# Attention and a squared-ReLU MLP on one core: score visits of three pieces in place of two

## The chip, the cores and the metric

The kernel runs on one core of one Trainium2 chip. The metric is the time of one execution on the device in microseconds (us), taken over several runs. The core has a matrix engine, TensorE (PE in the profile, with PEld for its weight loads), the elementwise engines VectorE (DVE) and ScalarE (ACT), GpSimd (POOL), and SyncE (SP). SP issues most of the DMAs here; POOL issues those of the first two batches and of the weights.

## The reference

Two operations are fused. The first is causal attention over 8 batches, 8 heads, 576 queries and head size 64, with 16 extra "beacon" keys and values in front that every query may see. The second is an MLP on the 4608 rows that come out of it.

```python
k_all = np.concatenate([beacon_k, k], axis=2)          # 592 keys
v_all = np.concatenate([beacon_v, v], axis=2)
scores = scale * np.matmul(q, k_all.transpose(0, 1, 3, 2))
causal[:, Nb:] = np.triu(np.ones((S, S), dtype=bool), k=1)
scores = np.where(causal, -1e9, scores)
a = softmax(scores);  attn = np.matmul(a, v_all)
x = attn.transpose(0, 2, 1, 3).reshape(4608, 512)
h = np.maximum(x @ w_in, 0.0)                          # 512 -> 2048
out = (h * h) @ w_out                                  # 2048 -> 512
```

## The kernel before

**Attention.** The 8 heads are taken as 4 pairs per batch; pair number p is 4b + pr. Keys stand on partitions, so a score matmul has only the 64 rows of one head as its contraction. The two heads of a pair lie in partitions 0 to 63 and 64 to 127 of `qT` and `kT`, and `emit_scores` (L607) issues their matmuls alternately. The causal part of a pair's scores is laid out as a stream of 1664 columns (`STREAM`, L547), the stream of a batch is 4 × 1664 = 6656 columns, and `PIECES` cuts it into 13 pieces of 512 columns.

A **strip** is a PSUM tile of 128 × 2 × 512 fp32, which is two banks, one for each head. A **score visit** is one stay of PE on scores: in batches 1 to 7 `new_visit` (L630) and `add_batch` (L641) make visits of two pieces, with both strips, and a last one of one piece, so seven visits for a batch. One ACT instruction (`add_exp`, L618) then takes the exponential of a whole strip, both heads together (1024 columns), into the bf16 buffer `pt`. DVE applies the causal mask with a minimum (`emit_mask`, L689 and L693), PE multiplies by the values (L715; a column of ones gives the row sum), and DVE divides (L732, L734) into `xn`. Batch 0 goes by another, finer path (`add_pair`).

`xn` is transposed into `xT`, by PE for batches 0 to 2 (L782) and by DMA for the rest (`add_xt`, L765).

**MLP.** It runs over 9 chunks of 512 rows. Stage 1 (L878) is, for each of 16 column groups, four matmuls of 512 columns into one PSUM bank; ACT (L894) or DVE (L896) applies the ReLU into `g`, and DVE squares (L903). Stage 2 (L916) is, for each of four groups of 128 rows, sixteen matmuls into one bank; the result is copied to `osb` (L316 or L318) and stored by SP (L944). For the last rows it is cut into three column ranges (L828).

**PSUM.** All eight banks are given out: two strips (four banks) and four single banks `ps`, which serve the MLP, the value matmuls (two at most) and the transposes (two at most).

**What sets the order.** No queue is written out by hand. `Order.run` (L69) is a planner that runs while the program is built: every piece of work is an `Op` with an engine, a duration, what it needs, what it takes from a pool of buffers (`take`) and gives back (`give`), a priority and sometimes a gate. The planner simulates the engines, always starts the available op of lowest priority number, and emits the instructions in that order. On the chip each engine runs its instructions strictly in that order and waits on semaphores. A visit has a gate (`gate_at`, L598): it prefers to wait until the MLP has come so far. When PE has nothing to do in the first 22 us of the plan, the planner puts in fillers (L286): matmuls on zeros whose result nobody reads, of 128 columns up to 4.0 us of the plan and of 256 columns after that (L139).

The lines that fix the shape of a visit:

```python
    qk = add(f"qk{b}.{n}", "PE", 0.2, emit, prio=100.0 * pos - 1000.0, take=("strip", "strip"), gate=gate_at(pos - SHIFT))
    ...
    if len(parts) == 2 or n == NPC - 1 and b not in CROSS:
        opened.clear()
```

**Loads.** Batches 0 and 1 are loaded by POOL's queue, in strided form, and transposed by PE (L472, L475). From batch 2 on SP loads q, k and v into eight staging buffers (L362), POOL casts to bf16 (L318), and two large DMA transposes on SP write `qT` and `kT` (L395). SP also issues the `xT` transposes (L765) and the stores (L944), all in one queue.

Of the kernel before, what the change touches and what calls it, by code (L numbers as in the profile page):

```python
# [11 lines left out]
AF = mybir.ActivationFunctionType  # L12
# [4 lines left out]
class Op:  # L17
# [1 line left out]

    __slots__ = ("name", "engs", "dur", "emit", "prio", "need", "users", "left", "ready",  # L20
                 "take", "give", "gate", "held", "slots", "dma", "pe_time", "behind", "followers",
                 "sync", "insts", "late")

    def __init__(self, name, engs, dur, emit, prio=0.0, deps=(), take=None, give=None,
                 gate=None, dma=0.0, pe_time=0.0, behind=(), sync=(), late=0.0):
        self.name = name
        self.late = late
        self.engs = engs if isinstance(engs, (tuple, list)) else (engs,)
        self.dur = dur
        self.emit = emit  # L30
        self.prio = prio
        self.sync = list(sync)
        self.need = list(deps) + self.sync
        self.users = []
        self.take = (*take, 1)[:3] if take else None
        self.give = give
        self.gate = gate
        self.held = None
        self.slots = []
        self.dma = dma  # L40
        self.pe_time = pe_time
        self.behind = list(behind)
        self.followers = []


class Order:
# [16 lines left out]
    def add(self, *a, **kw):  # L63
        op = Op(*a, **kw)
        op.need = [d for d in op.need if d is not None]
        self.ops.append(op)
        return op

    def run(self):  # L69
# [23 lines left out]
        now = 0.0  # L93
        while events:
            now = events[0][0]
            while events and events[0][0] <= now + 1e-9:
                _, _, kind, op = heapq.heappop(events)
                if kind in ("done", "done_pe"):
                    for u in op.users:
                        if ("PE" in u.engs) == (kind == "done_pe"):  # L100
                            u.left -= 1
                            if u.left == 0:
                                release(u)
                elif kind == "give":
                    from_op, which = op.give if isinstance(op.give, tuple) else (op.give, 0)
                    pool, cls = from_op.take[:2]
                    self.pools[pool].append(from_op.slots[which])
                    if cls in self.inuse:
                        self.inuse[cls] -= 1
            again = True  # L110
            while again:
                again = False
                for e in engines:
                    if free[e] > now + 1e-9:
                        continue
                    best = None
                    fallback = None
                    for op in avail[e]:
                        if any(free[x] <= now + 1e-9 for x in op.engs[:op.engs.index(e)]):
                            continue  # L120
                        if op.take:
                            pool, cls, need = op.take
                            if len(self.pools[pool]) < need:
                                continue
                            if cls in self.limits and self.inuse[cls] + need > self.limits[cls]:
                                continue
                        if op.gate is not None and not op.gate(self):
                            if fallback is None or op.prio < fallback.prio:
                                fallback = op
                            continue  # L130
                        if op.dma and len(lanes[e]) >= self.DEPTH[e] and lanes[e][-self.DEPTH[e]] > now + 1e-9:
                            continue
                        if best is None or op.prio < best.prio:
                            best = op
                    if best is None:
                        best = fallback
                    if best is None:
                        if e == "PE" and 0.3 < now < self.FILL_UNTIL and self.pools["ps"]:
                            cols = 128 if now < 4.0 else 256  # L139
                            free[e] = now + 0.107  # L140
                            issued.append((Op("fill", "PE", 0.107, lambda e, cols=cols, bank=self.pools["ps"][0]: self.fill(bank, cols)), e, now))
                            seq += 1
                            heapq.heappush(events, (free[e], seq, "free", None))
                        continue
# [8 lines left out]
                    if op.take:  # L153
                        pool, cls, need = op.take
                        op.slots = [self.pools[pool].pop(0) for _ in range(need)]
                        op.held = (pool, cls, op.slots[0])
                        if cls in self.inuse:
                            self.inuse[cls] += need
                    dur = op.dur[e] if isinstance(op.dur, dict) else op.dur
# [34 lines left out]
def kernel(  # L194
# [403 lines left out]
    def gate_at(pos):  # L598
        return lambda o: o.progress >= mlp_chunk_us * (LEAD + PACE * (pos - HP))
# [7 lines left out]
    def emit_scores(b, mms, st):  # L607
        for pr, c, t0, t1, at in mms:
            for hj in range(2):
                hp = slice(64 * hj, 64 * hj + 64)  # L610
                nc.tensor.matmul(  # L611
                    st[:, hj, at:at + t1 - t0],
                    kT[b % 2][hp, pr, 128 * c:128 * c + 128],
                    qT[b % 2][hp, pr, t0:t1],
                    start=True, stop=True,
                )

    def add_exp(name, qk, s, at, width, prio):  # L618
        def emit(e):
            nc.scalar.activation(pt[:, :, at:at + width], strips[qk.slots[s]][:, :, 0:width],  # L620
                                 AF.Exp, bias=0.0, scale=scale)

        return add(name, "ACT", 0.18 + 2 * width / 1200.0, emit, prio=prio, deps=[qk], give=(qk, s))

    exps_of = {}
    CROSS = ()
    SHIFT = 0.25
    opened = []

    def new_visit(b, n):  # L630
        pos = HP * b + 512.0 * n / PW
        parts = []

        def emit(e):
            for s, (bb, m) in enumerate(parts):
                emit_scores(bb, PIECES[m], strips[qk.slots[s]])

        qk = add(f"qk{b}.{n}", "PE", 0.2, emit, prio=100.0 * pos - 1000.0, take=("strip", "strip"), gate=gate_at(pos - SHIFT))
        opened.append((qk, parts))

    def add_batch(b):  # L641
        for pr in range(HP):
            p = HP * b + pr
            qk_ops[p], av_ops[p], exps_of[p] = [], [], []
        for n in range(NPC):
            if not opened:
                new_visit(b, n)
            qk, parts = opened[0]
            parts.append((b, n))
            qk.take = ("strip", "strip", len(parts))  # L650
            qk.dur += sum(t1 - t0 for _, _, t0, t1, _ in PIECES[n]) / 2400.0
            pairs = sorted({mm[0] for mm in PIECES[n]})
            e = add_exp(f"exp{b}.{n}", qk, len(parts) - 1, 512 * n, 512,
                        1.0e-2 * (HP * b + 512.0 * n / PW) - 30.0)
            for pr in pairs:
                p = HP * b + pr
                for o in deps_of(b, pr, 0) + av_ops[p - HP]:
                    if o not in qk.need:
                        qk.need.append(o)
                qk_ops[p].append(qk)  # L660
                exps_of[p].append(e)
            if len(parts) == 2 or n == NPC - 1 and b not in CROSS:
                opened.clear()
        for pr in range(HP):
            add_phase(b, pr, HP * b + pr, 0, WHOLE[pr][0], 100.0 * (HP * b + pr), exps_of[HP * b + pr])

    def add_pair(b, pr):
        p = HP * b + pr
        qk_ops[p], av_ops[p] = [], []
        for n, ph in enumerate(SPLIT):  # L670
            base = 20.0 * RANK.index((p, n))
            exps = []
            for i, (mms, off, width) in enumerate(ph.pieces):
                def emit_qk(e, mms=mms, box=(box := {})):
                    emit_scores(b, [(pr, *mm) for mm in mms], strips[box["qk"].slots[0]])

                qk = box["qk"] = add(f"qk{p}.{n}.{i}", "PE", 0.2 + sum(max(96, mm[2] - mm[1]) for mm in mms) / 2400.0, emit_qk,
                                     prio=base + i - 1000.0, deps=deps_of(b, pr, n), take=("strip", "strip"))
                qk_ops[p].append(qk)
                exps.append(add_exp(f"exp{p}.{n}.{i}", qk, 0, PW * p + off, width, (base + i) * 1.0e-4 - 400.0))  # L680
            add_phase(b, pr, p, n, ph, base, exps)

    def add_phase(b, pr, p, n, ph, base, exps):
# [364 lines left out]
```

The softmax here doesn't subtract the row's maximum and nothing guards it: scores larger than these inputs give would overflow.

## Time and profile before

| what | value |
|---|---|
| median of 8 runs | 341.02 us (340.63 to 343.6) |
| the profiled execution, its own time | 341.17 us |
| the profiled execution, its span | 339.4 us |
| PE busy | 335.1 us |
| ACT busy | 190.3 us |
| DVE busy | 170.5 us |
| POOL busy | 93.2 us |
| score matmuls (L611) | 596 |
| exponentials (L620) | 107 |

The time of a run is longer than the span of its profile by 1.8 us, which lie around the instructions. Busy is the time in which an engine had at least one instruction at work. Matmuls are pipelined, and the record of one reaches beyond the start of the next; so the useful length of a PE stretch is read from the start of its first matmul to the start of the first matmul of the next stretch.

### The profile page before, as it was taken

The numbers are of one execution on the slowest core, as the hardware profiler recorded it, in microseconds if no ns is written. First come the engines' busy times: TensorE is split into PE (matmuls) and PEld (weight loads), VectorE is DVE, ScalarE is ACT, GpSimd is POOL, SyncE is SP. The second block draws the span as 40 slices with busy tenths as digits, with TensorE's granted clock in tenths as the row PEclk, the third lists the DMA queues.
The fourth block names the chain that finished last, engine by engine and source line by source line (L and its number), as shares of the span: only waits on it lengthen the run. The fifth ranks groups of instructions, "written<-read, shape, count | busy, mean of one in ns | idle before, by whom it ended". The sixth has DMA issues, their size and how long they took to land.

```text
span 339.4 us, 7787 instructions
## 1 busy us (share of the span) xinstructions
PE 335.1 (99%) x3197; PEld 187.2 (55%) x3197; DVE 170.5 (50%) x389; ACT 190.3 (56%) x270; POOL 93.2 (27%) x145
## 2 busy tenths in 40 slices
PE   8999999999999999999999999999999999999996
PEld 7578765544554554554458845545555544444444
DVE  3786976147465973486236643766255502401400
ACT  3886765377638745575466654665277216514621
POOL 9874803416405514052415051403000000000000
PEclk9999999999999999999999999999999999999999
DMA  8999989999899999899989998996310131011003
GB/s 149 189 206 218 206 145 196 232 240 216 173 211 231 201 174 185 180 229 171 211 156 222 231 206 135 215 229 121 105 62 2 29 104 62 0 61 64 0 2 124
DMA packets 143953, 51.72 MB, mean 152 GB/s; under 512 B 130702, under 2 KB 138798, under 8 KB 143918
## 3 DMA queue, kind: packets, MB, share of 16 engines
q1 hardware_dynamic: 135375, 42.19, 62.2%
q0 software_dynamic: 7904, 8.69, 14.9%
q8 instruction: 25, 0.41, 0.5%
q10 hardware_dynamic: 639, 0.36, 0.4%
q14 instruction: 10, 0.08, 0.1%
HBM read 37.22 MB, written 9.44 MB: 137 GB/s over the span
## 4 chain that ended last, share of the span: by engine, by line
PE 98%; DVE 1%; issue 0%; ACT 0%; DVEq 0%
PE ps L878 37%; PE ps L916 36%; PE ps L715 9%; PE strip L611 9%; PE ps L286 3%; PE ps L475 1%; PE ps L782 1%; PE ps L828 1%; DVE g L903 1%; PE ps L472 0%; PE ps L420 0%; DVE g L896 0%; ACT osb L316 0%; DVE g L292 0%; DVE qT L318 0%
## 5 line engine op out<-in xcount | busy, mean ns | idle before, releaser
L878 PE MATMUL ps<-xT,w_in 128*128 128x512 bf16 (+3 forms) x704 | 134.0, 340 | 0.1
L916 PE MATMUL ps<-w_out,g 128*128 128x512 bf16 x560 | 131.5, 379 | 0.0
L620 ACT ACTIVATE pt<-strip 128x1024 bf16<-128x1024 f32 (+3 forms) x107 | 101.9, 999 | 42.9 <-PE strip L611 42.5
L878 PEld LDWEIGHTS <-w_in 128*128 128x128 bf16 x704 | 65.5, 98 | 52.3 <-issue 1.4
L894 ACT ACTIVATE g<-ps 128x512 bf16<-128x512 f32 (+2 forms) x120 | 67.6, 563 | 43.9 <-PE ps L878 43.2
L903 DVE TENSOR_TENSOR g<-g 128x1024 bf16<-128x1024 bf16 (+2 forms) x80 | 52.6, 663 | 68.7 <-ACT g L894 67.8
L916 PEld LDWEIGHTS <-g 128*128 128x128 bf16 x560 | 51.0, 98 | 54.8 <-issue 1.7
L318 POOL CAST qk_area<-stg 128x512 bf16<-128x512 f32 (+2 forms) x60 | 41.7, 702 | 66.6 <-DMA stg<-in_q_dram 32.9
L316 ACT COPY osb<-ps 128x512 f32<-128x512 f32 (+2 forms) x28 | 15.8, 568 | 50.8 <-PE ps L916 48.6
L318 POOL CAST vb<-stg 128x512 bf16<-128x512 f32 (+1 forms) x40 | 25.5, 645 | 66.0 <-DMA stg<-in_v_dram 48.4
L715 PEld LDWEIGHTS <-pt 128*128 128x128 bf16 (+1 forms) x960 | 35.7, 98 | 11.0 <-issue 1.9
L715 PE MATMUL ps<-vb,pt 128*128 128x65 bf16 (+1 forms) x960 | 39.8, 194 | 0.0
L689 DVE TENSOR_TENSOR pt<-pt,tri 128x512 bf16<-128x512 bf16 x64 | 30.3, 483 | 10.5 <-ACT pt L620 9.4
L611 PE MATMUL strip<-qT,kT 64*128 64x208 bf16 (+15 forms) x596 | 34.2, 239 | 0.0
L734 DVE TENSOR_TENSOR xn<-ps,rcp 128x320 bf16<-128x320 f32 (+2 forms) x64 | 31.5, 492 | 2.3
L611 PEld LDWEIGHTS <-kT 64*128 64x128 bf16 x596 | 19.0, 94 | 21.2 <-issue 19.7
L732 DVE RECIPROCAL rcp<-ps 128x5 f32<-128x5 f32 (+2 forms) x64 | 12.2, 191 | 36.3 <-PE ps L715 36.2
L896 DVE TENSOR_SCALAR g<-ps 128x512 bf16<-128x512 f32 (+2 forms) x40 | 23.4, 602 | 8.4 <-PE ps L878 7.5
L318 DVE COPY osb<-ps 128x512 f32<-128x512 f32 (+1 forms) x10 | 6.5, 652 | 30.6 <-PE ps L916 15.2
L286 PE MATMUL ps<-g 128*128 128x256 bf16 (+1 forms) x83 | 11.8, 299 | 1.1 <-DVE warm L293 1.1
L362 POOL DMA_DIRECT2D stg<-in_v_dram x10 | 8.6, 866 | 5.8 <-DMA w_in<-in_moe_w_in_dram 4.2
L286 PEld LDWEIGHTS <-g 128*128 128x128 bf16 x83 | 7.8, 121 | 3.3 <-issue 1.4
(40 smaller groups left out, 82.5 us busy)
## 6 DMA issues: line engine op xcount, KB each, us to landing
out_dram<-osb SPq DMA_DIRECT2D x17, 512.0 KB, 4.2
stg<-in_q_dram SPq DMA_DIRECT2D x24, 256.0 KB, 4.9
stg<-in_k_dram SPq DMA_DIRECT2D x18, 256.0 KB, 5.2
stg<-in_v_dram SPq DMA_DIRECT2D x18, 256.0 KB, 4.8
w_in<-in_moe_w_in_dram POOLq DMA_DIRECT2D x4, 512.0 KB, 7.9
w_out<-in_moe_w_out_dram POOLq DMA_DIRECT2D x4, 512.0 KB, 10.8
stg<-in_v_dram POOLq DMA_DIRECT2D x6, 256.0 KB, 7.6
stg<-in_k_dram SPq DMA_DIRECT2D x6, 224.0 KB, 4.2
```

What stands on the lines that cost most here:

```text
L286: nc.tensor.matmul(ps[bank][:, 0:cols], g[1][:, 0, 0:128], g[1][:, 0, 0:cols], start=True, stop=True)
L318: eng[e].tensor_copy(dst, src)
L611: nc.tensor.matmul(st[:, hj, at:at + t1 - t0], kT[b % 2][hp, pr, 128 * c:128 * c + 128], qT[b % 2][hp, pr, t0:t1], start=True, stop=True,)
L620: nc.scalar.activation(pt[:, :, at:at + width], strips[qk.slots[s]][:, :, 0:width], AF.Exp, bias=0.0, scale=scale)
L689: nc.vector.tensor_tensor(out=d, in0=d, in1=tri[:, m0:m0 + m, :][:, None].to_broadcast([128, 2, m, 128]), op=ALU.min)
L715: nc.tensor.matmul(a[:, at + (t - tl[0]) * (D + 1):at + (t - tl[0] + 1) * (D + 1)], P[0:rr, hj, o:o + 128], vb[b % 2][0:rr, c, 2 * pr + hj ...
L734: nc.vector.tensor_tensor(out=xn[b % 2].rearrange("p t (h d) -> p h t d", d=D)[:, h0:h0 + nh, tl[0]:tl[0] + nt], in0=a[:, :, :, 0:D], in1= ...
L878: nc.tensor.matmul(h[:, lo - spans[0][0]:hi - spans[0][0]], w_in_sb[:, mc, ft * 128:(ft + 1) * 128], xT[:, mc, lo % RING:lo % RING + hi - lo],
L894: nc.scalar.activation(dst, h, AF.Relu, bias=0.0, scale=1.0)
L896: nc.vector.tensor_scalar(out=dst, in0=h, scalar1=0.0, scalar2=None, op0=ALU.max)
L903: nc.vector.tensor_tensor(out=d, in0=d, in1=d, op=ALU.mult)
L916: nc.tensor.matmul(o, G[:, fc, ts * 128:(ts + 1) * 128], w_out_sb[:, fc, :], start=(fc == 0), stop=(fc == NFT - 1))
```

## The change

1. **Visits of three pieces.** `PLAN` gives the sizes: 2, 2, 3, 3, 3 pieces in batches 1 and 2; 2, 3, 3, 3, 2 in batches 3 to 7. That is five visits for a batch where there were seven. A visit of three has more than the strips hold: its first piece goes into any two free `ps` banks, one for each head (`wide`), and its other two pieces into the two strips. It is two ops on PE, the second straight behind the first.
2. **Exponentials.** The piece in `ps` banks has two exponentials of 512 columns, one for each head; a piece in a strip has one of 1024, as before.
3. **Order of visits.** From batch 3 on, and for visits of three in batches 1 and 2, a visit stands behind the one before it.
4. **Fillers.** The limit below which fillers have 128 columns moves from 4.0 to 7.0 us of the plan.

The number of score matmuls and their columns, the masks, the value matmuls and the MLP are the same. The planner plans anew with these ops, so the order of other instructions moves too. The diff, without the declarations of the new fields and with the batch-0 path cut:

```diff
                 elif kind == "give":
                     from_op, which = op.give if isinstance(op.give, tuple) else (op.give, 0)
+                    if which < 0:
+                        self.pools["ps"].append(from_op.wide[which])
+                        continue
...
                         if op.take:
                             pool, cls, need = op.take
-                            if len(self.pools[pool]) < need:
+                            if len(self.pools[pool]) < need or held and pool == "ps":
+                                continue
+                            if op.wide and len(self.pools["ps"]) < 2:
                                 continue
...
-                            cols = 128 if now < 4.0 else 256
+                            cols = 128 if now < 7.0 else 256
...
                         op.slots = [self.pools[pool].pop(0) for _ in range(need)]
                         op.held = (pool, cls, op.slots[0])
+                        if op.wide:
+                            op.wide = [self.pools["ps"].pop(0) for _ in range(2)]
...
                 nc.tensor.matmul(
-                    st[:, hj, at:at + t1 - t0],
+                    st[hj][:, at:at + t1 - t0],
...
-    CROSS = ()
     SHIFT = 0.25
-    opened = []
...
+    PLAN = ((2,2,3,3,3),(2,2,3,3,3),(2,3,3,3,2),(2,3,3,3,2),(2,3,3,3,2),(2,3,3,3,2),(2,3,3,3,2))
+    FREE = 2
+    last_qk = []
...
-        for n in range(NPC):
-            if not opened:
-                new_visit(b, n)
-            qk, parts = opened[0]
-            parts.append((b, n))
-            qk.take = ("strip", "strip", len(parts))
...
+        for size in PLAN[b - 1]:
+            pos = HP * b + 512.0 * n / PW
+            box = {}
+            runs = [(0,), (1, 2)] if size == 3 else [tuple(range(size))]
+            for k, run in enumerate(runs):
+                def emit(e, run=run, n=n, box=box, size=size):
+                    for s in run:
+                        if size == 3 and s == 0:
+                            emit_scores(b, PIECES[n], [ps[x] for x in box["qk"].wide])
+                        else:
+                            st = strips[box["qk"].slots[s - (size == 3)]]
+                            emit_scores(b, PIECES[n + s], [st[:, 0, :], st[:, 1, :]])
+
+                qk = add(f"qk{b}.{n + run[0]}", "PE", 0.2 / len(runs) + 512 * len(run) / 2400.0, emit,
+                         prio=-1.0e6 if k else 100.0 * pos - 1000.0, behind=[qk] if k else last_qk[-1:] if size == 3 or b > FREE else [],
+                         take=None if k else ("strip", "strip", min(size, 2)), gate=None if k else gate_at(pos - SHIFT))
...
+                    if size == 3 and s == 0:
+                        es = []
+                        for hj in range(2):
+                            def emit_half(e, hj=hj, at=at, qk=qk):
+                                nc.scalar.activation(pt[:, hj, at:at + 512], ps[qk.wide[hj]], AF.Exp, bias=0.0, scale=scale)
+
+                            es.append(add(f"exp{b}.{n}.{hj}", "ACT", 0.18 + 512 / 1200.0, emit_half, prio=prio + 1.0e-4 * hj, deps=[qk],
+                                          give=(qk, hj - 2)))
+                    else:
+                        es = [add_exp(f"exp{b}.{n + s}", box["qk"], s - (size == 3), at, 512, prio, qk)]
```

More of the change, by code (lines that the diff above doesn't have):

```diff
@@ L21 @@
                  "take", "give", "gate", "held", "slots", "dma", "pe_time", "behind", "followers",
-                 "sync", "insts", "late")
+                 "sync", "insts", "late", "wide")
     def __init__(self, name, engs, dur, emit, prio=0.0, deps=(), take=None, give=None,
@@ L27, in __init__ @@
         self.late = late
+        self.wide = []
         self.engs = engs if isinstance(engs, (tuple, list)) else (engs,)
@@ L117, in run @@
                     fallback = None
+                    held = False
                     for op in avail[e]:
@@ L616, in emit_scores, with add_exp @@
                 )
-    def add_exp(name, qk, s, at, width, prio):
+    def add_exp(name, qk, s, at, width, prio, done):
         def emit(e):
@@ L621, in emit @@
                                  AF.Exp, bias=0.0, scale=scale)
-        return add(name, "ACT", 0.18 + 2 * width / 1200.0, emit, prio=prio, deps=[qk], give=(qk, s))
+        return add(name, "ACT", 0.18 + 2 * width / 1200.0, emit, prio=prio, deps=[done], give=(qk, s))
     exps_of = {}
-    CROSS = ()
     SHIFT = 0.25
-    opened = []
[L630 to L639, printed above, removed]
+    PLAN = ((2,2,3,3,3),(2,2,3,3,3),(2,3,3,3,2),(2,3,3,3,2),(2,3,3,3,2),(2,3,3,3,2),(2,3,3,3,2))
+    FREE = 2
+    last_qk = []
     def add_batch(b):
@@ L644, in add_batch @@
             qk_ops[p], av_ops[p], exps_of[p] = [], [], []
-        for n in range(NPC):
-            if not opened:
-                new_visit(b, n)
-            qk, parts = opened[0]
-            parts.append((b, n))
-            qk.take = ("strip", "strip", len(parts))
[L651 to L663, printed above, removed]
+        n = 0
@@ new lines, in add_batch @@
+        for size in PLAN[b - 1]:
[13 more added lines that the diff above has]
+                         take=None if k else ("strip", "strip", min(size, 2)), gate=None if k else gate_at(pos - SHIFT))
+                last_qk.append(qk)
+                if k == 0:
+                    qk.wide = [None] if size == 3 else []
+                    box["qk"] = qk
+                for s in run:
+                    at, prio = 512 * (n + s), 1.0e-2 * (pos + 0.1 * s) - 30.0
+                    if size == 3 and s == 0:
[7 more added lines that the diff above has]
+                        es = [add_exp(f"exp{b}.{n + s}", box["qk"], s - (size == 3), at, 512, prio, qk)]
+                    for pr in sorted({mm[0] for mm in PIECES[n + s]}):
+                        p = HP * b + pr
+                        for o in deps_of(b, pr, 0) + av_ops[p - HP]:
+                            if o not in box["qk"].need:
+                                box["qk"].need.append(o)
+                        qk_ops[p].append(qk)
+                        exps_of[p] += es
+            n += size
@@ L664, in add_batch @@
+        assert n == NPC
         for pr in range(HP):
@@ L674, in emit_qk @@
                 def emit_qk(e, mms=mms, box=(box := {})):
-                    emit_scores(b, [(pr, *mm) for mm in mms], strips[box["qk"].slots[0]])
+                    st = strips[box["qk"].slots[0]]
+                    emit_scores(b, [(pr, *mm) for mm in mms], [st[:, 0, :], st[:, 1, :]])
                 qk = box["qk"] = add(f"qk{p}.{n}.{i}", "PE", 0.2 + sum(max(96, mm[2] - mm[1]) for mm in mms) / 2400.0, emit_qk,
@@ L679, in add_pair @@
                 qk_ops[p].append(qk)
-                exps.append(add_exp(f"exp{p}.{n}.{i}", qk, 0, PW * p + off, width, (base + i) * 1.0e-4 - 400.0))
+                exps.append(add_exp(f"exp{p}.{n}.{i}", qk, 0, PW * p + off, width, (base + i) * 1.0e-4 - 400.0, qk))
             add_phase(b, pr, p, n, ph, base, exps)
```

## The prediction, made before the changed kernel was run

> **What bounds the kernel now.** I read the page's busy shares first, then who waited for whom, then the timeline of PE around visits. On the page:
>
> ```profile
> PE 335.1 (99%) x3197; PEld 187.2 (55%) x3197; DVE 170.5 (50%) x389; ACT 190.3 (56%) x270; POOL 93.2 (27%) x145
> ```
>
> PE is busy for 335.1 of 339.4 us and the next engine for 56%. A busy share alone isn't proof, since matmul records overlap; the list of waits settles it. PE's matmuls have one wait in it, 1.1 us at the very start, but the weight loads of the score line have an odd one:
>
> ```profile
> PEld L611 <- issue: 19.7, 52, 0.4
> ```
>
> Before 52 score groups the weight load stood for 0.2 to 0.4 us and waited for nothing that the profile shows. What that costs PE is in its timeline:
>
> ```profile
> 104.83 1.03 PE L878 MATMUL ps<-xT,w_in 128*128 128x512 bf16 x4
> 105.79 0.62 PE L611 MATMUL strip<-qT,kT 64*128 64x96 bf16 x12
> 106.34 2.76 PE L878 MATMUL ps<-xT,w_in 128*128 128x512 bf16 x12
> 109.04 0.61 PE L611 MATMUL strip<-qT,kT 64*128 64x192 bf16 x12
> 109.59 1.90 PE L878 MATMUL ps<-xT,w_in 128*128 128x512 bf16 x8
> 111.32 0.62 PE L715 MATMUL ps<-vb,pt 128*128 128x65 bf16 x15
> 111.78 1.03 PE L878 MATMUL ps<-xT,w_in 128*128 128x512 bf16 x4
> ...
> 118.89 0.40 PE L611 MATMUL strip<-qT,kT 64*128 64x96 bf16 x8
> 119.22 1.90 PE L878 MATMUL ps<-xT,w_in 128*128 128x512 bf16 x8
> ```
>
> Take starts to starts. Eight MLP matmuls before a value group take 111.32 - 109.59 = 1.73 us, 0.216 each. Four before a score visit take 105.79 - 104.83 = 0.96 instead of 0.864: going into a visit costs 0.10. A visit of one piece lasts 119.22 - 118.89 = 0.33, one of two pieces 0.55, so a further piece costs 0.22 and coming out costs 0.33 - 0.22 = 0.11. A visit has a fixed cost of about 0.21 us, whatever it holds. Going into and out of the value matmuls shows no such cost.
>
> **What the Trainium skill says.** "TensorEngine Tiling (Array Packing)", section Key Properties: "Changing tiling mode (not just tile) drains the TensorE". Score matmuls use 64 rows, MLP and value matmuls 128; the trace agrees, with 0.10 in and 0.11 out. "PSUM — Partial Sum Buffer", section Specifications (TRN2): eight banks of 512 fp32 values per partition; the two strips and four single banks use all eight, so a third piece can only borrow single banks. Whether borrowing makes anyone wait no trace of before shows.
>
> **Part 1, five visits for seven.** In batches 1 to 7 there are 49 visits and then 35; in the order of the changed program PE has the same 596 score matmuls in 14 fewer stretches. Within a visit of three, the seam between single banks and strips is no change of mode. 14 × 0.21 = 2.95 us off a path on which PE never waits after some 41 us. Bounds: 14 × 0.20 = 2.8 and 14 × 0.225 = 3.15 (a first MLP matmul after a visit takes 0.01 longer).
>
> **Part 2, the halves of the exponential.** Of one piece in each of 21 visits, one exponential (1.023 us for 1024 columns in the groups by form) becomes two of 512. The nearest row is the ReLU of the same 128x512 out of PSUM on ACT, 0.597. Thus 21 × (2 × 0.597 - 1.023) = 3.6 us more on ACT, 190.3 to 193.9, which PE's 335 us cover. The cover has to hold locally. From the start of such a visit the first piece is done by about 0.10 + 0.22 + 0.1 = 0.4; if ACT is free, the two halves end at 1.0 and 1.6 and give their banks back, and the strips at 2.6 and 3.7. (a) PE leaves the visit at 0.86 with two single banks free and fills them until 2.6 with MLP units of 0.864; the third unit needs the bank of the first half, 1.6 us earlier. (b) The next visit needs both strips. In the changed order the closest one comes after sixteen MLP matmuls, at 0.86 + 3.46 = 4.3, so 0.6 us to spare, one ACT instruction. Both hold on paper, (b) narrowly. The densest stage is batch 3:
>
> ```profile
> 102.50:121.60 19.10, 19.10 (x198) 9.81 (x197) 15.49 (x31) 15.19 (x20) 10.93 (x15) 1.00 1.18 210
> ```
>
> The columns are PE, PEld, DVE, ACT and POOL: 81% and 80% for DVE and ACT, and PE did not wait. With the same work, 0.5 us more on ACT and a stage 0.5 us shorter, ACT comes to 84%. I take 0.2 us for waits of PE in all, bounds 0 and 2 (0.1 for each of the 21).
>
> **Part 3, what else moves.** The order of PE is the same up to the third visit of batch 1, apart from the filler widths; after that value groups and MLP units change places at no cost of their own. On SP a few stores and q/k loads swap places, and the five `xT` transposes of batch 4, some 6.4 us of issue, now stand ahead of the last three v loads of batch 5. These land that much later, near 174; in the changed order the first value group of batch 5 moves from 171.4 to about 178, so it is covered. q/k loads of batch 6 behind them keep their place: the same instructions stand ahead of them but for one store. The key transposes land 1.1 us (batch 6) to 3.8 us (batch 2) before the first visit of their batch. In the changed order, with PE never waiting, the smallest margin is again batch 6, about 1.0. The tail from the last value group on is the same.
>
> **Part 4, fillers.** They change in one place, on PE's chain:
>
> ```profile
> 5.25 2.37 PE L286 MATMUL ps<-g 128*128 128x256 bf16 x15
> 7.46 0.46 PE L472 MATMUL ps<-ident,qk_area 112*128 112x112 bf16 x6
> ...
> 30.14 0.70 PE L475 MATMUL ps<-ident,qk_area 96*64 96x96 bf16 x24
> ```
>
> From 5.25 to 7.46 these 15 take 2.21 us, 0.147 each: some of them at half clock. A 128-column filler at half clock takes 0.107 (the seven from 3.76 to 4.51). For full clock I use 0.056, the price of N=128 in "TensorE: Matmul & The Clock Gate", section "Wait — 56ns, not 53.3ns?"; no row here has it. With 0.213 and 0.107 for the wide ones, 5.7 were slow, so the clock rose near 6.45. After the change 11 slow ones and 4 fast ones: 1.2 + 0.2 = 1.4 us, 0.8 less. The casts that L472 needs ended at 5.84, so PE is ahead by 0.8 and its followers with it. It does not keep that. The 24 transposes at 30.14 need the keys of batch 1, whose DMA is issued at 19.13 by POOL, behind the weights, and lands 10.7 us later, at 29.8. PE comes there at 29.3 and waits: 0.3 remains of 0.8. Bounds: 0 (the clock rises later, or DVE, which decides around 38 to 40.7 with its squares, takes it) and 0.8 (the DMA comes earlier too).
>
> **The sum.** Against the profiled execution: span 339.4 - 2.95 - 0.3 + 0.2 = 336.35, plus 1.8 around it is 338.1; its own time was 341.17, 0.15 over the median of 341.02. So 338.0 for the median.
>
> **The rivals.** (A) *A part goes into new waits.* ACT and DVE are both over 80% in the dense stages, so a ReLU or a strip is sometimes late; or a transpose of batch 6 lands a microsecond later and PE stands before its visit. For: margins of 0.6 and 1.0 us. Against: PE did not wait once in such stages before. Price 1 to 2 us: about 339.4.
>
> (B) *The visit's cost is not removed but shifted*, for instance because a third piece pays at the seam what an entry paid, 21 × 0.13 = 2.7 us. Against: all matmuls of a visit are of the same mode, and a second piece pays nothing beyond its columns. Time near 340.7.
>
> (C) *Slower: the MLP starves for single banks.* In each visit of three, two of the four are held. If ACT is inside a 1.02 us exponential and a ReLU when the piece is ready, the halves end at 2.6 to 3.2 and the third MLP unit, due at 2.6, waits up to 0.6, and the next visit with it. It needs 3.25 / 21 = 0.155 us a visit to eat the gain, 0.20 to be measurably slower; at 0.4 a visit it gives 338.0 + 8.2 = 346.2. For: ACT runs exponentials ahead of ReLUs by the planner's priorities. Against: DVE takes ReLUs as well, and the planner starts nothing without free banks, with ACT times close to the trace's.
>
> **How the numbers follow.** 338.0 has a chance of 0.66, with its own range of 337.1 (start gain 0.8, entry 0.225) to 338.8. A has 0.19, B 0.07, C 0.08. The range for 8 in 10 reaches from 337.1 to 339.7, which takes in most of A. What this kernel's measurement can tell from no change is 0.3%, or 1.0 us: below 340.0 is faster, above 342.0 slower. Forecast and A give 0.85 faster, B 0.07 the same, C 0.08 slower.
>
> **What would show it.** Right: 14 fewer score stretches with 0.10 and 0.11 at their ends, a three-piece visit of about 0.77 from start to start; no PE wait after 41 us; the transposes of 30.14 at 29.8 to 29.9; ACT near 194. Wrong: MLP matmuls after a three-piece visit with steps over 0.23 (A, C), a seam inside visits (B), or score weight loads that wait for a DMA or ACT instead of "issue".

## The result and the profile after

| | before | after |
|---|---|---|
| median | 341.04 us (32 runs) | 337.98 us (11 runs) |
| span of the profiled execution | 339.4 us | 336.3 us |
| ratio after to before | | 0.9906, 95% interval [0.989, 0.9922] |

The change makes the kernel 3.06 us faster; 338.0 was forecast. Two executions of the experiments below are left out of their ratios: one of E1 that had a mean granted clock of 0.722 (442.85 us, the only one of E1 with a profile) and one of E10 (1188.56 us). First the busy shares on the page of the changed kernel, with two of its groups and one line of its waits:

```profile
PE 331.6 (99%) x3197; PEld 188.8 (56%) x3197; DVE 168.6 (50%) x389; ACT 191.3 (57%) x291; POOL 91.7 (27%) x145
```

```profile
L629 ACT ACTIVATE pt<-strip 128x1024 bf16<-128x1024 f32 x70 | 68.2, 1033 | 8.9 <-PE strip L620 8.9
...
L671 ACT ACTIVATE pt<-ps 128x512 bf16<-128x512 f32 x42 | 22.8, 597 | 13.7 <-PE ps L620 11.1 <-issue 2.6
```

```profile
PEld L620 <- issue: 14.2, 38, 0.4
```

PE has the same 3197 matmuls and is busy for 3.5 us less. ACT has 21 instructions more and 1.0 us more to do. The weight loads of the score line, now L620, stand before 38 groups where it was 52: 14 fewer, and 5.5 us less of such standing in all. PE's timeline around two visits of three pieces, where the first group of each goes into single banks (`ps`) and the second into strips:

```profile
105.14 0.59 PE L901 MATMUL ps<-xT,w_in 128*128 128x512 bf16 x2
105.67 0.40 PE L620 MATMUL ps<-qT,kT 64*128 64x96 bf16 x6
105.90 0.61 PE L620 MATMUL strip<-qT,kT 64*128 64x128 bf16 x12
106.44 3.63 PE L901 MATMUL ps<-xT,w_in 128*128 128x512 bf16 x16
110.00 0.40 PE L620 MATMUL ps<-qT,kT 64*128 64x224 bf16 x6
110.23 0.60 PE L620 MATMUL strip<-qT,kT 64*128 64x256 bf16 x10
110.77 0.63 PE L738 MATMUL ps<-vb,pt 128*128 128x65 bf16 x15
```

From start to start a visit of three lasts 0.77 us (105.67 to 106.44). Its first piece takes 0.23 including the way over to the strips, hardly more than a piece's 0.22: no cost at the seam. The sixteen MLP matmuls after it take 3.56 up to the next visit, 16 times 0.216 and 0.10 for going in. Matmul by matmul, from 41 us to the end, the trace of the changed kernel has no wait of PE over 0.2 us; the three over 0.02 us are 0.12 at a value matmul (50.28) and 0.13 and 0.20 before transposes of `xn`, where the kernel before has two of the same kind (0.19 and 0.13).

At the start the narrow fillers did what was forecast, and then most of the lead was lost (PE's timeline again):

```profile
5.25 1.65 PE L295 MATMUL ps<-g 128*128 128x128 bf16 x15
6.74 0.46 PE L481 MATMUL ps<-ident,qk_area 112*128 112x112 bf16 x6
...
13.68 0.37 PE L620 MATMUL strip<-qT,kT 64*128 64x208 bf16 x4
14.54 0.45 PE L484 MATMUL ps<-ident,qk_area 96*64 96x96 bf16 x12 [0.48 <-DMA qk_area<-in_k_dram]
```

The 15 fillers take 1.49 us from start to start, and PE is ahead by 0.72, soon 0.88, of the execution before. At 14.54 it stands for the keys of the last pair of batch 0 (the bracket is idle time and who ended it). After that it is 0.32 ahead. It waits for keys or queries twice more around 30 and 34 us, each time for 0.2 or less; its first visit of batch 1 starts at 33.52, 0.18 ahead of the execution before, and its second at 38.20, 0.04 *behind*. A second profiled execution of the changed kernel (`after_again`, below) went another way:

```profile
29.48 0.70 PE L484 MATMUL ps<-ident,qk_area 96*64 96x96 bf16 x24 [0.49 <-DMA qk_area<-in_k_dram]
...
40.44 1.03 PE L901 MATMUL ps<-xT,w_in 128*128 128x272 bf16 x8 [0.35 <-DVE g L919]
```

There PE waits first at 29.48, for the keys of batch 1, starts the first visit of batch 1 at 33.04, 0.66 ahead of the kernel before, and loses that at 40.44, where it waits for DVE. Both executions reach the first stage-2 matmul within 0.07 us of each other (44.46 and 44.39).

### The profile page after: what moved, and what is told of

Same layout as the page of the kernel before. It is cut to its first block, busy times and chain, and to the rows that moved or that the text cites. A ratio compares the mean times of both kernels' runs of the same rounds, so it can differ in the third digit from the quotient of the medians.

```text
span 336.3 us, 7856 instructions
## 1 busy us (share of the span) xinstructions
PE 331.6 (99%) x3197; PEld 188.8 (56%) x3197; DVE 168.6 (50%) x389; ACT 191.3 (57%) x291; POOL 91.7 (27%) x145
## 4 chain that ended last, share of the span: by engine, by line
PE 90%; DMA 5%; POOL 3%; issue 0%; ACT 0%; POOLq 0%
PE ps L939 36%; PE ps L901 36%; PE ps L738 8%; PE strip L620 5%; DMA qk_area<-in_k_dram 3%; DMA stg<-in_v_dram 2%; PE ps L620 2%; POOL qk_area L449 1%; PE ps L851 1%; PE ps L484 1%; PE ps L805 1%; POOL vb L327 1%; POOL stg L371 1%; POOL w_in L830 0%; POOL tri L311 0%; POOL stg L370 0%
## 5 line engine op out<-in xcount | busy, mean ns | idle before, releaser
L917 ACT ACTIVATE g<-ps 128x512 bf16<-128x512 f32 (+2 forms) x118 | 66.3, 562 | 42.4 <-PE ps L901 41.9
L629 ACT ACTIVATE pt<-strip 128x1024 bf16<-128x1024 f32 (+3 forms) x86 | 81.4, 1002 | 13.2 <-PE strip L620 13.0
L939 PEld LDWEIGHTS <-g 128*128 128x128 bf16 x560 | 51.5, 98 | 56.9 <-issue 1.7
L327 POOL CAST qk_area<-stg 128x512 bf16<-128x512 f32 (+2 forms) x60 | 40.0, 676 | 64.1 <-DMA stg<-in_k_dram 36.3
L738 PE MATMUL ps<-vb,pt 128*128 128x65 bf16 (+1 forms) x960 | 38.9, 194 | 0.0
L919 DVE TENSOR_SCALAR g<-ps 128x512 bf16<-128x512 f32 (+2 forms) x42 | 24.8, 606 | 14.0 <-PE ps L901 13.4
L671 ACT ACTIVATE pt<-ps 128x512 bf16<-128x512 f32 x42 | 22.8, 597 | 13.7 <-PE ps L620 11.1
L620 PEld LDWEIGHTS <-kT 64*128 64x128 bf16 x596 | 19.8, 94 | 16.0 <-issue 14.2
L620 PE MATMUL strip<-qT,kT 64*128 64x208 bf16 (+13 forms) x474 | 27.0, 239 | 0.0
L295 PE MATMUL ps<-g 128*128 128x128 bf16 (+1 forms) x83 | 10.9, 292 | 1.1 <-DVE warm L302 1.1
```

The costliest lines, as they stand in the source:

```text
L327: eng[e].tensor_copy(dst, src)
L620: nc.tensor.matmul(st[hj][:, at:at + t1 - t0], kT[b % 2][hp, pr, 128 * c:128 * c + 128], qT[b % 2][hp, pr, t0:t1], start=True, stop=True,)
L671: nc.scalar.activation(pt[:, hj, at:at + 512], ps[qk.wide[hj]], AF.Exp, bias=0.0, scale=scale)
L738: nc.tensor.matmul(a[:, at + (t - tl[0]) * (D + 1):at + (t - tl[0] + 1) * (D + 1)], P[0:rr, hj, o:o + 128], vb[b % 2][0:rr, c, 2 * pr + hj ...
L917: nc.scalar.activation(dst, h, AF.Relu, bias=0.0, scale=1.0)
L919: nc.vector.tensor_scalar(out=dst, in0=h, scalar1=0.0, scalar2=None, op0=ALU.max)
```

## The experiments

**The two parts, each alone.** E1 is the kernel before with the narrow fillers; E2 is the changed kernel with the old limit.

```diff
# e1_fill_only, on the kernel before
-                            cols = 128 if now < 4.0 else 256
+                            cols = 128 if now < 7.0 else 256
# e2_visits_only, on the changed kernel
-                            cols = 128 if now < 7.0 else 256
+                            cols = 128 if now < 4.0 else 256
```

> The kernel before with the narrow fillers alone. Theory (what fillers gain at the start is taken back where PE waits for the keys of batches 0 and 1): between 0 and -0.3 us against before, that is a ratio of 0.999 to 1.000. Rival (the fillers carry a good part of the gain, since PE starts 0.8 us earlier): -0.8 us, ratio 0.9977.

> The changed visits with the fillers of before. Theory (14 visits fewer at 0.21 us): -2.95 us against before, ratio 0.9913, span near 336.4. Rival (fillers carry a part): -2.2 us, ratio 0.9935.

E1: 341.12 against 341.05 us, ratio 0.9997 [0.9981, 1.0012]. E2: 338.22 us, ratio 0.9908 [0.9883, 0.9932]. So the visits bring the gain, and the fillers nothing that can be measured: a gain of up to 0.6 us isn't excluded by E1's interval, which holds the forecast's 0.3 as well as zero.

**The count of visits.** Two kernels with the changed code and other plans:

```diff
-    PLAN = ((2,2,3,3,3),(2,2,3,3,3),(2,3,3,3,2),(2,3,3,3,2),(2,3,3,3,2),(2,3,3,3,2),(2,3,3,3,2))
# e3_seven
+    PLAN = ((2, 2, 2, 2, 2, 2, 1),) * 7
# e4_nine
+    PLAN = ((2, 1, 2, 1, 2, 1, 2, 1, 1),) * 7
# e10_three_and_one
+    PLAN = ((3, 1, 3, 1, 3, 1, 1),) * 7
```

> The changed program with seven visits of 2, 2, 2, 2, 2, 2 and 1 pieces in each batch, so 49 again. Theory (the count of visits decides): the time of before, within 0.3 us. Rival (the order of visits or the new planning brings the gain): it keeps 1 us or more of the 3 us.

> The changed program with nine visits a batch, 2, 1, 2, 1, 2, 1, 2, 1 and 1 pieces, 63 in all. Theory (0.21 us a visit, in a straight line): 14 x 0.21 = 2.95 us more than before, ratio 1.0087, and 5.9 us more than the changed kernel. Rival (fewer visits help only since buffers turn over better): shorter visits ask less of the strips at a time, so no more than before, ratio 1.000.

E3: 341.27 us, ratio 1.0 [0.9984, 1.0017]: with 49 visits the gain is gone. E4: 343.53 us, ratio 1.0063 [1.004, 1.0086], so 5.55 us over the changed kernel for 28 visits more, 0.20 each. Over the kernel before it is 2.48 us for 14 visits more, where 2.95 was expected. The rival, which had shorter visits cost nothing, falls.

Whole times carry the noise of the start. In eleven profiles, of kernels whose PE order is the same up to there but for filler widths, the first visit of batch 1 starts between 33.04 and 34.61 us, which depends on how long PE waits for keys (1.7 us in e6_dummy64) and on when the granted clock rises (between 4.35 and 6.86 us in the ten traces that show it). A stretch without that is the one from the first stage-2 matmul to the last matmul of the kernel:

| kernel | visits in the stretch | its length, us |
|---|---|---|
| after (two executions) | 32 | 288.63, 288.97 |
| e2_visits_only | 32 | 288.96 |
| before | 45 | 291.27 |
| e3_seven | 45 | 291.28 |
| e4_nine | 57 | 293.76 |

From 32 to 45 visits the line rises by (291.27 - 288.63) / 13 = 0.20 us each (0.18 with 288.97), and from 45 to 57 by 0.21. The stretches hold the same matmuls, but for one score piece in e4_nine that stands ahead of its stretch (0.21 us; with it the second rise is 0.23).

**Three-piece visits without fewer visits.** E10 keeps the 21 visits with borrowed banks and has 49 visits all the same.

> The changed kernel with visits of 3, 1, 3, 1, 3, 1 and 1 pieces in each batch: as many three-piece visits with borrowed banks as in the changed kernel (21), but 49 visits in all as before. Theory (the count decides, borrowing neither gains nor costs): the time of the kernel before, 341.0, within 0.4 us. Rival (a piece in single banks with exponentials by head is a gain in itself, since it frees its buffers sooner): 1 us or more under it. Rival (borrowing costs PE waits that the changed order hides): 1 us or more over it.

339.80 us, ratio 0.9961 [0.9927, 0.9996]: 1.0 us faster than before by the medians, 1.3 by the ratio, where the theory said 0.4 at most and the first rival 1 or more. Its stretch has 44 visits and 290.27 us, 0.8 below the line. The trace places that: 0.43 are score matmuls, two pieces, that stand ahead of its stretch and not in it, and 0.3 are the two waits before the transposes of `xn` that the kernel before has and this one hasn't. Ahead of the stretch, from the first visit of batch 1 on, it takes 11.35 us with these two pieces and one visit more, 0.62 us of scores, and the kernel before 11.22 without them. The kernel before waits 0.29 there at 40.75, before an MLP matmul, and goes once more into key transposes and out of them, 0.19 (a price that comes below). So E10 gains waits and one change of work, and each of its visits costs what it did before. Another order of the same work can shift the time by about a microsecond. That borrowing itself removes those waits isn't likely: the changed kernel borrows as often and has the waits before `xn`.

**What the cost of a visit is.** E5 and E6 put one more matmul of 64 columns inside each three-piece visit, between its first and second piece, once with 128 rows and once with 64 (the edit of E5 is shown; E6 has `slice(0, 64)` for both `slice(0, 128)`):

```diff
                 def emit(e, run=run, n=n, box=box, size=size):
+                    if size == 3 and run[0] == 1:
+                        nc.tensor.matmul(strips[box["qk"].slots[0]][:, 0, 0:64], ident[slice(0, 128)], ident[slice(0, 128), 0:64], start=True, stop=True)
```

> The changed kernel with one more matmul in each of the 21 three-piece visits, between its first and its second piece: 128 rows, 64 columns, on the identity, into a strip bank that the scores overwrite. Theory (a change between 64 and 128 rows costs 0.10 to 0.11 each way): 21 x (0.21 + 0.03) = 5.0 us more than the changed kernel, about 343.0. Rival (the cost belongs to starting a group of scores from other work, its weight loads or its semaphores): only the columns, 21 x 0.03 = 0.6 us, about 338.6.

> The same extra matmul in the same place with 64 rows. Theory: no change of mode, so only its own columns, 21 x 0.03 = 0.6 us more than the changed kernel, about 338.6, and 4.4 us less than with 128 rows. Rival (any foreign matmul breaks the stream): the same as with 128 rows.

E5: 342.48 us, 4.5 more than the changed kernel (ratio to before 1.0047 [1.0027, 1.0067]). E6: 338.21 us, 0.2 more (0.9926 [0.9898, 0.9954]). PE's timeline of E5, and then of E6:

```profile
106.58 0.39 PE L620 MATMUL ps<-qT,kT 64*128 64x96 bf16 x6
106.90 0.20 PE L652 MATMUL strip<-ident 128*128 128x64 bf16 x1
107.04 0.62 PE L620 MATMUL strip<-qT,kT 64*128 64x128 bf16 x12
107.59 3.63 PE L903 MATMUL ps<-xT,w_in 128*128 128x512 bf16 x16
```

```profile
106.84 0.40 PE L620 MATMUL ps<-qT,kT 64*128 64x96 bf16 x6
107.07 0.19 PE L652 MATMUL strip<-ident 64*128 64x64 bf16 x1
107.07 0.63 PE L620 MATMUL strip<-qT,kT 64*128 64x128 bf16 x12
107.63 3.63 PE L903 MATMUL ps<-xT,w_in 128*128 128x512 bf16 x16
```

With 128 rows the way from the first piece to the strips takes 107.04 - 106.58 = 0.46 us, with 64 rows 0.23, as in the changed kernel. The extra matmul with 64 rows isn't free for all that: the second head's matmuls behind it start 0.025 later, and the visit is that much longer. Over the 21 visits the median from start to start is 0.769 us in the changed kernel, 0.795 with the extra 64 rows and 1.011 with 128. The first adds 0.026, the time of 64 columns (64/512 of an MLP matmul's 0.216 is 0.027), the second 0.24. So a foreign matmul in the middle of a visit costs its columns, and 128 rows among 64 cost 0.22 more. By the whole times the two kernels differ by 4.27 us, 0.20 for each of 21 visits.

Not every change of rows costs this. In the trace before, from 20 us on, these are the medians of what a step takes over its columns, beside matmuls of 128 rows and 128 columns of weights:

| other matmuls | going in, us | coming out, us |
|---|---|---|
| scores, 64 rows | 0.098 | 0.095 |
| beacon transposes, 16 rows (one place) | 0.098 | 0.090 |
| key and query transposes, 96 rows, 64 columns | 0.096 | 0.098 |
| last value matmuls, 80 rows | 0.002 | 0.006 |
| transposes of `xn`, 112 rows | 0.008 | 0.010 |

**Taking the covers away.** E7 runs the halves of the exponential after the strips, so the single banks come back some two microseconds later; the planner moves visits too. E8 cuts the strips' exponentials of these visits in two as well, for the same data in more instructions.

```diff
# e7_halves_last
-                for s in run:
-                    at, prio = 512 * (n + s), 1.0e-2 * (pos + 0.1 * s) - 30.0
+                for s in ((1, 2, 0) if k else ()) if size == 3 else run:
+                    at, prio = 512 * (n + s), 1.0e-2 * (pos + 0.1 * (s or 3)) - 30.0
# e8_split_strips
+        cut = width == 512 and len(qk.wide) > 0
...
-            nc.scalar.activation(pt[:, :, at:at + width], strips[qk.slots[s]][:, :, 0:width],
+            for hj in range(2) if cut else (slice(0, 2),):
+                nc.scalar.activation(pt[:, hj, at:at + width], strips[qk.slots[s]][:, hj, 0:width],
```

> The changed kernel with the two half exponentials after those of the strips, so that the two single banks are held to about 3.7 us after the start of a visit and not to 1.0 and 1.6. Theory (in the changed kernel the third MLP unit finds its bank 1.6 us early): with this cover taken away that unit is up to 1.0 us late; planned around in part, 0.3 us for each of 21 visits, 6 us more, about 344. Rival (single banks are not scarce, even two are enough): no change, 338.0.

> The changed kernel with the strips' exponentials of three-piece visits cut in two as well: 42 more ACT instructions, 7.2 us more on ACT, planned as if they were not there. The last strip of a visit then comes free at 4.0 us in place of 3.7, with the next visit at 4.3. Theory (ACT is covered with 0.6 us to spare at the narrowest place): no more than 0.5 us, below 338.5. Rival (ACT paces the dense stages): a third or more of the 7.2 us shows, 340.4 or above.

E7: 344.34 us, 6.4 more than the changed kernel (ratio to before 1.0099 [1.0076, 1.0121]). PE's timeline at the first three-piece visit, and its list of waits:

```profile
41.42 0.60 PE L620 MATMUL strip<-qT,kT 64*128 64x224 bf16 x12
41.96 1.05 PE L901 MATMUL ps<-xT,w_in 128*128 128x272 bf16 x8
43.62 1.03 PE L901 MATMUL ps<-xT,w_in 128*128 128x272 bf16 x8 [0.61 <-DVE g L919]
44.95 0.62 PE L901 MATMUL ps<-xT,w_in 128*128 128x272 bf16 x4 [0.30 <-DVE g L919]
```

```profile
PE ps L901 <- DVE g L919: 1.7, 5, 0.6
PE strip L620 <- DMA kT<-qk_area: 1.6, 2, 1.2
```

After the visit PE fills two single banks (eight MLP matmuls) and stands 0.6 us until DVE's ReLU has emptied one of them, since the other two are still held. This is rival C of the prediction, made real by another order on ACT and the plan that follows from it. Steps that are too long by less than the list shows add up too: matmul by matmul, from 41 us on, the waits come to 7.8 us, where the changed kernel has 0.4. Of them 1.7 are waits for key transposes, which the moved visits meet earlier; the others stand before work that takes single banks, and which of them are for a bank and which for its data the list doesn't tell.

E8: 338.21 us, ratio 0.9927 [0.9897, 0.9956], 0.2 more than the changed kernel and within its noise. ACT is busy for 193.7 us, 2.4 more and not 7.2, and in the trace the strips come free 3.53 to 3.64 us after the start of a dense visit, 0.12 later than in the changed kernel. So E8 shows that this much is covered, not how much more would be.

**Fewer visits still.** If a visit costs 0.2 us, visits across the border of two batches should gain. E9 and E9b cut batches 3 to 7 as one stream, 32 visits in all, with the single visit of two at its end or at its start; the changed kernel ran beside them once more.

```diff
-    PLAN = ((2,2,3,3,3),(2,2,3,3,3),(2,3,3,3,2),(2,3,3,3,2),(2,3,3,3,2),(2,3,3,3,2),(2,3,3,3,2))
+    SIZES = (2,2,3,3,3) * 2 + (3,) * 21 + (2,)      # e9b: ... + (2,) + (3,) * 21
...
-        for size in PLAN[b - 1]:
+        for n in range(NPC):
+            i = NPC * (b - 1) + n
+            if i in STARTS:
+                size = STARTS[i]
```

> The changed kernel with batches 3 to 7 as one stream of 65 pieces, cut into 21 visits of three and a last one of two, so that some visits hold the last pieces of a batch and the first of the next: 32 visits in place of 35. Theory (0.21 us a visit and nothing else): 3 x 0.21 = 0.63 us less than the changed kernel, about 337.4, ratio to the kernel before 0.989. Rival (a visit across batches waits for the keys of the next batch, and the last value groups of its batch come late): PE waits before such visits, or buffers turn over later; no gain or up to 2 us more, 338 to 340.

> The same with the visit of two pieces at the start of batch 3 and 21 visits of three after it, which puts the borders of batches at other places in the visits. Theory: as the other, about 337.4. Rival: as the other; if the two differ by over 0.5 us, where the borders fall decides and not the count.

> The changed kernel itself, on the same chip and in the same rounds as the two with visits across batches, to compare with: 338.0 us, ratio 0.991.

The changed kernel: 338.63 us, ratio 0.9924 [0.9911, 0.9937]. E9: 346.08 us, 1.0133 [1.0112, 1.0154]. E9b: 345.91 us, 1.0145 [1.0124, 1.0166]. Both are 7 us slower than the changed kernel, more than the rival said. PE's timeline of E9, and its busy times by stretch (columns: PE, PEld, DVE, ACT, POOL, then the granted clock):

```profile
141.79 1.09 PE L752 MATMUL ps<-vb,pt 128*128 128x65 bf16 x30 [0.62 <-DVE pt L726]
147.59 1.87 PE L915 MATMUL ps<-xT,w_in 128*128 128x512 bf16 x4 [4.71 <-DMA xT<-xn]
```

```profile
140.00:148.00 8.00, 2.50 (x54) 1.80 (x53) 3.90 (x13) 3.53 (x5) 2.45 (x4) 0.91 0.93 165
148.00:156.00 8.00, 8.00 (x52) 4.15 (x51) 2.38 (x6) 2.57 (x5) 0.00 (x0) 0.66 0.82 185
```

The last piece of batch 3 now waits for batch 4, at 128.6 us in place of 118.8. Its value matmuls, its rows of `xn` and their transposes come later, and the MLP, which had used up what there was, stands 4.7 us for them. The granted clock is at half from 146.63 to 153.46, so the 8 us from 148 on run at a mean of 0.66; an estimate of what this costs is half of the time from 147.59 to 153.46, 2.9 us.

## Why the prediction was right

1. *Five visits for seven, 2.95 us.* Right in mechanism and size. In the trace before, steps into scores cost 0.098 and out of them 0.095 over their columns, and the changed kernel has 14 fewer of each: 14 × 0.193 = 2.70. From start to start the visits of a batch last 3.40 us in place of 3.61, which is 0.106 for each of the two that are gone; with 0.098 for going in and 0.011 for the slower first MLP matmul behind a visit it is 0.21 each. By the whole times E3 against E2 gives 0.22, E4 0.18 to 0.20, E5 against E6 0.20. The drain that the Trainium skill states for a change of tiling mode ("TensorEngine Tiling (Array Packing)", section Key Properties) fits what a visit costs: E5 adds it inside a visit by rows alone.
2. *No cost at the seam* (against rival B). Right: 0.23 us for the first piece, and E6.
3. *ACT, 3.6 us more, covered.* Covered in the changed kernel. The term was too large: ACT is busy 1.0 us more. Back to back two halves take 1.08 us and a strip's exponential 0.97, since their records overlap, so the halves added 22.8 - 21 × 0.97 = 2.4; two 512-column ReLUs more fell to DVE, which takes 1.2 off again.
4. *Waits in the dense stages, 0.2 us.* About right: 0.1 at 50.28, in both profiled executions, and in the second one 0.3 more, at 184 and 209 us. The two margins were real. For the strips 0.6 us was forecast; in the trace the smallest is 0.81 (visit at 131.4), and E8, which takes 0.12 of it, costs nothing that can be measured. For the single banks 1.6 us was forecast, and E7, which takes two microseconds, makes PE wait. Neither experiment tells which of the two is narrower.
5. *SP's order and the transposes.* Nothing waits for them in the changed kernel.
6. *Fillers, 0.3 us.* Not decided. The fillers saved 0.72 us where 0.8 was forecast: the clock rose at 6.63, not near 6.45, so 13 of them were slow and not 11. In `after_again` it rose at 5.70 and they saved 1.17; at full clock they stand 0.056 apart, as the prediction had it. The path was right in one profiled execution of two: in `after_again` PE waits first at the keys of batch 1, as forecast, and then for DVE, which the lower bound allowed for; in the other, keys of batch 0 that landed later took most of the lead at 14.5 us. E1 can't tell 0.3 us from zero.

The profiled execution is 3.10 us shorter than the one before: 0.18 ahead of the first visit of batch 1, 0.28 from there to the first stage-2 matmul, with one visit fewer, and 2.64 behind it, with 13 fewer. That the visits carry nearly all of it is shown. That the sum came within 0.1 us is luck in part: two executions of the changed kernel differ by 0.34 us in that last stretch alone, so the two small terms, 0.3 of fillers and 0.2 of waits, could not be checked by it.

## What to carry to other kernels

Find in the trace which changes between kinds of matmuls cost PE time, count them and multiply; here it is 0.2 us for a there and back between 64 and 128 rows, and nothing like it between 80 or 112 and 128. Work of one kind is then worth collecting as far as the buffers allow. Buffers borrowed for that must be given back first: which exponentials run first, with the plan that follows from it, decided between 3 us of gain and 3 us of loss. And collect only work that nobody waits for: the last piece of a batch had a transpose and the whole MLP behind it.

## What the runs showed of the hardware

- The cost of the change between 64 and 128 rows is nearly symmetric, 0.098 us in and 0.095 us out, whichever kind of 128-row work stands at the other side (MLP or values). Transposes with 16 rows, or with 96 rows and 64 columns, have it as well (0.090 to 0.098); 80 and 112 rows with 128 columns don't (0.010 or less).
- A 64-row matmul of 64 columns added in a stream of 64-row matmuls cost 0.026 us, its columns (E6), while one of 128 rows cost 0.24 (E5).
- In E9, after 4.7 us without a matmul, the granted clock was 0.66 over the next 8 us. In E9b it was at half from 144.90 to 151.73, though the longest stand in its list is 2.35 us.
- The first visit of batch 1 starts between 33.04 and 34.61 us in executions whose PE order is the same up to there, which bounds what a change at the start can be worth.
